# Layer 0 of a two-layer transformer in chunks of 2, 4, 4, 4 and 2 tiles, with held-back first loads and longer transfer latencies in the scheduler's model

## The chip, the cores and the metric

The kernel runs on one core of one Trainium2 chip. The metric is device time in microseconds (us) of one execution. A profile is one execution recorded by the hardware profiler. The engines carry these names in it: PE is TensorE doing matmuls, PEld is TensorE loading weights (the two overlap), DVE is VectorE, ACT is ScalarE, POOL is GpSimd, SP is SyncE. A name such as SPq means the instruction queue of that engine.

## The reference

Two layers, each with sliding-window attention and a feed-forward block, both behind a layer norm. There are 2048 tokens (16 tiles of 128), width 576, 32 heads of 18, a window of 256 keys and a feed-forward width of 4608. Both layers use the same weights, which are read in bfloat16.

```python
def _A_ref(x, wqkv, wo):                       # attention, H = 32, Dh = 18, W = 256
    q, k, v = split((x @ wqkv))
    scores = einsum("bhqd,bhkd->bhqk", q, k) * Dh ** -0.5
    mask = (i - j >= 0) & (i - j < W)
    p = softmax(where(mask, scores, -1e9))
    return (p @ v) @ wo
def _B_ref(x, w1, b1, w2, b2):                 # feed-forward
    return gelu(layernorm(x) @ w1 + b1) @ w2 + b2

x = x + _A_ref(_layernorm(x), wqkv, wo)        # layer 0
x = x + _B_ref(_layernorm(x), ...)
x = x + _A_ref(_layernorm(x), wqkv, wo)        # layer 1
x = x + _B_ref(_layernorm(x), ...)
```

## The kernel before

The kernel walks through chunks of four tiles, four chunks a layer, eight in all. In the step of chunk k, the attention of chunk k and the feed-forward of chunk k - 1 are written side by side, so that TensorE has feed-forward matmuls to do while ScalarE works on the exponentials of the attention.

```python
CH = [(l, t, 4) for l in range(NL) for t in range(0, NT, 4)]     # (layer, first tile, tiles)
...
for k in range(NK + 1):
    b = 4 * k                                      # a lower number is a higher priority
    if not last:
        if 0 < k < NK - 1: ln1(k + 1, b + 1)       # layer norm and transposes for the next qkv
        E(k, range(0, 4), b - 0.5)                 # attention, first half of the heads
    if k >= 2: mm2(k - 2, 1, b); w2_load(0, b + 1) # second-layer matmuls, two chunks back
    if k >= 1: G_part(k - 1, 0, b + 1)             # first-layer matmuls and gelu, first half
    if not last: E(k, range(4, 8), b + 1.5)
    if k >= 1: mm2(k - 1, 0, b + 2); w2_load(1, b + 3)
    if not last:
        ... qkv(k + 1, i, b + 2.2 + 0.2 * i) ...
        tail(k, b + 1.9)                           # transposes of the attention, output projection
    if k >= 1: G_part(k - 1, 1, b + 3)
```

This text does not fix the order in which an engine executes. Every `add(...)` makes a task with an engine, a `cost` (time on the engine), a `lat` (further time until its result may be read) and a priority. A list scheduler plays the program through on a model of the engines and writes one fixed order for each engine. On the chip an engine keeps this order and waits on semaphores where a result isn't there yet. So a wrong `lat` makes nothing incorrect; it makes the model believe that an instruction will not have to wait.

```python
# Plan.schedule, cut
for e in ENGS:
    for t in released[e]:
        st = max(free[e], t.ready)
        ...
        key = (round(st, 3), t.prio, t.idx)        # the earliest start wins, then the priority
...
t.end = st + t.cost + t.lat
s.ready = max(s.ready, st + t.cost + (t.lat if data and not same else 0.0))
```

Scores and first-layer matmuls keep the order of the text among themselves (`fifo="pa"`), and so do exp and gelu on ScalarE (`fifo="act"`). Second-layer matmuls, qkv and the output projection are free: they are the filler that the scheduler can put anywhere.

The parts that the change touches: the transposes, which are DMAs from on-chip memory to on-chip memory, issued by SyncE; the masks on GpSimd; and the loads at the start.

```python
# layer norm -> xnTa or xnTm; q and k -> qT and kT; attention -> attT
add("sp", lambda e: e.dma_start_transpose(dst[...], xn[:, sl, :]), ..., dma="t", cost=1.3, lat=1.4, prio=prio)
add("sp", lambda e, ...: e.dma_start_transpose(dst, qn[:, sl, :]), ..., dma="t", cost=1.3, lat=1.4, prio=prio)
add("sp", lambda e, i=i: e.dma_start_transpose(attT[...], attq[:, i, :]), ..., dma="t", cost=1.3, lat=1.4, prio=prio - 0.1)

# scores: one unit is four heads against up to 512 query columns; two exps, then the masks
add("act", lambda e, h2=h2: e.activation(pT[:, sl, 2*h2:2*h2+2, lo:hi], two(bs[h2])[:, :, lo:hi], ACT.Exp, scale=SCALE), ..., fifo="act")
ap = pT[:, sl, :, col:col + nb * 128]
add("pool", lambda e, ...: e.affine_select(ap, ap, pattern=pat, ...), ...)

# start: all weights and all of x at once; x as bfloat16, then 16 casts to the float32 residual
x_load(0, n0, [], 4.0, -10)
for n, w in enumerate("qkv"):
    dma("act", wqkv[...], A_wqkv[...], lat=7.0 + 3 * n, prio=-10, fifo="act")
for a in range(n0, NT, 4):
    x_load(a, min(4, NT - a), ["wkA"], ...)
dma("act", wo_sb[...], A_wo[...], lat=14.0, ...)
...
for t in range(NT):
    add("pool", lambda e, t=t: e.tensor_copy(x_res[:, t, :], x_in[:, t, :]), reads=[f"xin{t}"], writes=X(t), cost=0.7, ...)
for _ in range(NB1):
    w1_load(0, [f"q{n0 - 1}"])
w2_load(0, 0, [f"q{n0 - 1}"])
```

The softmax here doesn't subtract the row's maximum and nothing guards it: scores larger than these inputs give would overflow.

## Time and profile before

| | before |
|---|---|
| time, median of the first 3 runs | 1006.06 us (1005.98 to 1006.28) |
| span of the profiled run | 1007.7 us |
| TensorE busy | 927.4 us, 92% |
| first qkv matmul, first scores, first feed-forward matmul | 15.0, 34.0, 133.4 us |
| TensorE waits for the attention transposes | 16.8 us |
| moved by DMA | 126.60 MB |

From the page of the kernel before: busy time of each engine with its share of the span and its instruction count, then four rows in 40 slices of 25.2 us. A digit is the busy share in tenths; PEclk is the granted TensorE clock in tenths of full speed.

```profile
PE 927.4 (92%) x9312; PEld 584.9 (58%) x9312; DVE 311.9 (31%) x771; ACT 586.2 (58%) x705; POOL 378.4 (38%) x519
PE   3596799899999999899998999999999999999998
ACT  0356568577753777447761687627774377852531
PEclk9786799999999999999998999999999999999999
DMA  9925220974268251881628633484517725074540
```

TensorE bounds the kernel: from the sixth slice on its row is nearly all nines. The first five slices are different, with low digits and a low clock. That is the ramp. The windows view of the kernel before splits it. The columns are the stretch, its length, busy us (and instructions) of PE, PEld, DVE, ACT and POOL, the granted clock, the mean share of DMA engines in use, and GB/s.

```profile
0.00:34.00 34.00, 17.14 (x120) 12.47 (x121) 20.40 (x54) 1.28 (x1) 22.22 (x41) 1.00 1.24 231
34.00:80.00 46.00, 28.96 (x402) 18.70 (x402) 22.57 (x62) 27.26 (x37) 24.15 (x35) 0.78 0.53 142
80.00:92.00 12.00, 8.38 (x134) 4.97 (x134) 2.88 (x8) 8.56 (x12) 8.02 (x12) 0.53 0.62 88
92.00:120.00 28.00, 19.34 (x194) 11.68 (x195) 15.24 (x36) 13.36 (x14) 19.52 (x26) 0.65 0.43 85
120.00:160.00 40.00, 39.22 (x401) 23.18 (x400) 9.79 (x24) 28.57 (x35) 10.25 (x14) 1.00 0.23 65
```

Before 120 us TensorE is idle in part, and what it does runs at 0.53 to 0.78 of its clock for 86 us. A busy PE is therefore not enough as a measure. This document uses **lost time**: the length of a stretch minus the matmul work done in it, each matmul priced at its rate when TensorE runs without gaps. The prices come from the trace: 144 second-layer matmuls of 288 columns back to back took 17.64 us (0.1225 us each), 90 first-layer ones of 512 columns took 19.43 us (0.216 us), and other shapes are priced the same way by their columns (the 20-column value matmuls at 0.026 us, and the scores, four at a time on 32 rows each, at a quarter). Lost time adds up idle time and slow clock. It is an estimate, but with the same prices for every run. The kernel before loses 67.7 us by 130 us, a further 10.8 by 240 us, and 63.1 us in the 768 us after that.

The waits view of the kernel before, TensorE only. A line reads: what waited (written tile, source line), what ended the wait, us in all, times, longest. Line 519 is a qkv or output-projection matmul, 589 a score matmul, 598 an exp, 636 a value matmul, 619 a mask.

```profile
PE ps L519 <- DMA xnTa<-xn: 25.3, 4, 15.0
PE ps L519 <- DMA attT<-attq: 16.8, 9, 3.6
PE ps L589 <- ACT pT L598: 12.2, 22, 1.3
PE ps L636 <- POOL pT L619: 3.8, 5, 1.0
```

The second line is 16.8 us in nine waits, and it lies in the stage where TensorE is the bottleneck. One of the nine in the timeline of the kernel before (start, us, what, with the idle time before it in brackets):

```profile
298.38 0.29 PE L525 MATMUL ps<-wqkv,xnTa 128*128 128x288 bf16 x1
300.87 0.66 PE L519 MATMUL ps<-wo_sb,attT 128*128 128x288 bf16 x4 [2.19 <-DMA attT<-attq]
```

TensorE ends a qkv matmul and then sits for 2.19 us in front of the output projection, because the order says that the projection is next. The transpose needed 2.6, 3.2 and 5.9 us (least, median, most) from its issue to landing. The model has `cost` 1.3 and `lat` 1.4, together 2.7 us: nearly the least of the three.

### The profile page before, as it was taken

Reading aid. Unit: us, or ns where it says so; the run is one execution under the profiler, and the core shown is the slowest. Engines: PE = TensorE matmul, PEld = TensorE weight load, DVE = VectorE, ACT = ScalarE, POOL = GpSimd, SP = SyncE. Lnnn points to the kernel's source line nnn. Section 1 sums busy time; section 2 is a strip of 40 time slices with the busy share of each in tenths; the row PEclk is TensorE's granted clock in tenths of the full one; section 3 lists DMA queues with packets and bytes.
Section 4 is the critical chain, followed back from the end, with each engine's and each line's share of the span. In section 5 each row is a group of like instructions: output and inputs, shape, how many; then the busy total and the mean of one; then the engine's idle time right before and its main releaser. Section 6 shows DMA issues by size and latency. Waiting matters only on the chain.

```text
span 1007.7 us, 22352 instructions
## 1 busy us (share of the span) xinstructions
PE 927.4 (92%) x9312; PEld 584.9 (58%) x9312; DVE 311.9 (31%) x771; ACT 586.2 (58%) x705; POOL 378.4 (38%) x519
## 2 busy tenths in 40 slices
PE   3596799899999999899998999999999999999998
PEld 2363556556565656656575565755566565656556
DVE  4742611342136211534036130361114410132001
ACT  0356568577753777447761687627774377852531
POOL 8445724354333434425153161533333342541000
PEclk9786799999999999999998999999999999999999
DMA  9925220974268251881628633484517725074540
GB/s 252 273 45 89 54 72 25 199 187 131 72 150 164 75 163 39 180 184 41 183 70 170 148 108 94 120 177 103 166 48 170 143 66 183 25 194 122 184 129 25
DMA packets 226757, 126.60 MB, mean 126 GB/s; under 512 B 141792, under 2 KB 226528, under 8 KB 226656
## 3 DMA queue, kind: packets, MB, share of 16 engines
q1 hardware_dynamic: 219456, 122.20, 49.0%
q10 hardware_dynamic: 2432, 2.65, 0.9%
q0 software_dynamic: 4768, 0.31, 0.8%
q8 instruction: 74, 1.21, 0.5%
q14 instruction: 27, 0.22, 0.1%
HBM read 90.10 MB, written 2.36 MB: 92 GB/s over the span
## 4 chain that ended last, share of the span: by engine, by line
PE 68%; DMA 4%; DVE 3%; ACT 3%; issue 1%; POOL 1%; SPq 0%; DVEq 0%
PE ps L737 26%; PE ps L712 24%; PE ps L519 6%; PE ps L636 6%; PE ps L589 4%; DMA attT<-attq 3%; ACT pT L598 2%; PE ps L525 1%; DVE x_res L670 1%; DMA xnTm<-xn 1%; POOL rstd L460 1%; DVE xn L470 1%; ACT hT L716 1%; DVE st_all L447 0%; ACT L753 0%
## 5 line engine op out<-in xcount | busy, mean ns | idle before, releaser
L619 POOL TENSOR_SCALAR_AFFINE_SELECT pT<-pT 128x512 bf16<-128x512 bf16 (+1 forms) x368 | 278.1, 778 | 409.6 <-ACT pT L598 385.3
L598 ACT ACTIVATE pT<-ps 128x1024 bf16<-128x1024 f32 (+2 forms) x384 | 347.2, 971 | 133.6 <-PE ps L589 132.2
L716 ACT ACTIVATE hT<-ps,b1col 128x512 bf16<-128x512 f32 x288 | 196.6, 687 | 262.6 <-PE ps L712 262.4
L737 PE MATMUL ps<-w_sb,hT 128*128 128x288 bf16 x2304 | 314.2, 286 | 6.7 <-DVE x_res L670 5.6
L712 PE MATMUL ps<-xnTm,w_sb 128*128 128x512 bf16 x1440 | 320.1, 379 | 0.1
L737 PEld LDWEIGHTS ps<-w_sb,hT 128*128 128x128 bf16 x2304 | 210.3, 97 | 80.7 <-issue 20.5
L712 PEld LDWEIGHTS ps<-xnTm,w_sb 128*128 128x128 bf16 x1440 | 139.6, 98 | 158.6 <-issue 0.2
L670 DVE TENSOR_TENSOR x_res<-ps,x_res 128x288 f32<-128x288 f32 x160 | 71.0, 450 | 399.9 <-PE ps L737 362.4
L519 PE MATMUL ps<-wqkv,xnTa 128*128 128x288 bf16 x768 | 127.7, 297 | 29.7 <-DMA xnTa<-xn 25.3
L636 PEld LDWEIGHTS ps<-vA,pT 128*128 128x128 bf16 x2880 | 94.4, 96 | 29.1 <-issue 11.2
L519 PEld LDWEIGHTS ps<-wqkv,xnTa 128*128 128x128 bf16 x768 | 73.1, 101 | 58.5 <-issue 18.8
L636 PE MATMUL ps<-vA,pT 128*128 128x20 bf16 x2880 | 100.5, 172 | 5.3 <-POOL pT L619 3.8
L589 PE MATMUL ps<-qT,kT 32*128 32x384 bf16 (+2 forms) x1408 | 76.5, 285 | 18.7 <-ACT pT L598 12.2
L555 DVE CAST qn<-ps 128x288 bf16<-128x288 f32 x128 | 57.0, 452 | 55.2 <-PE ps L525 50.0
L519 PE MATMUL ps<-wo_sb,attT 128*128 128x288 bf16 x256 | 45.9, 313 | 16.8 <-DMA attT<-attq 16.8
L525 PE MATMUL ps<-wqkv,xnTa 128*128 128x288 bf16 x192 | 56.8, 296 | 0.0
L589 PEld LDWEIGHTS ps<-qT,kT 32*128 32x128 bf16 x1408 | 22.6, 93 | 53.9 <-issue 30.0
L694 POOL TENSOR_TENSOR x_res<-x_res,b2bc 128x576 f32<-128x576 f32 x32 | 45.0, 1409 | 15.1 <-DVE xn L470 13.9
L673 DVE TENSOR_TENSOR xn<-ps,x_res 128x288 bf16<-128x288 f32 x32 | 14.6, 457 | 114.7 <-PE ps L737 114.7
L470 DVE TENSOR_SCALAR xn<-x_res,mv_all,rstd 128x576 bf16<-128x576 f32 x60 | 43.1, 723 | 22.1 <-POOL rstd L460 10.4
L458 POOL TENSOR_SCALAR vtmp<-mv_all 128x1 f32<-128x1 f32 (+1 forms) x43 | 8.6, 200 | 103.6 <-DVE mv_all L449 101.2
L519 PEld LDWEIGHTS ps<-wo_sb,attT 128*128 128x128 bf16 x256 | 26.2, 106 | 30.7 <-DMA attT<-attq 20.6
(29 smaller groups left out, 281.5 us busy)
## 6 DMA issues: line engine op xcount, KB each, us to landing
w_sb<-in_B_w_dram SPq DMA_DIRECT2D x144, 288.0 KB, 5.2
w_sb<-in_B_w_dram SPq DMA_DIRECT2D x72, 512.0 KB, 4.2
w_sb<-in_B_w_dram SPq DMA_DIRECT2D x72, 64.0 KB, 3.9
hT<-in_A_x_dram SPq DMA_DIRECT2D x4, 576.0 KB, 6.3
out_dram<-xn SPq DMA_DIRECT2D x16, 144.0 KB, 1.8
wqkv<-in_A_wqkv_dram ACTq DMA_DIRECT2D x3, 576.0 KB, 7.4
wo_sb<-in_A_wo_dram ACTq DMA_DIRECT2D x1, 576.0 KB, 9.6
xnTa<-xn SPq DMA_TRANSPOSE x32, 3.9
```

Source lines behind the costliest of these rows:

```text
L470: add("dve", lambda e: e.tensor_scalar(xn[:, sl, 0:D], s[:, t, :], mv_all[:, t, 0:1], rstd[:, t:t + 1], op0=ALU.subtract, op1=ALU.mult), r ...
L519: ins = e.matmul(bank(bs[o])[:, 0:n], lhs(o, c, full), rhs(o, c, full), start=(c == 0), stop=False)
L525: ins = e.matmul(bank(bs[o])[:, 0:n], lhs(o, 4, full), rhs(o, 4, full), start=False, stop=True)
L555: add("dve", lambda e, o=o, b=bs[o], qv=qv: e.tensor_copy(qv[:, o * 16:(o + 1) * 16, 0:DH], bank(b)[:, 0:HB].rearrange("p (h d) -> p h d", ...
L589: ins = e.matmul(two(bs[j // 2])[:, j % 2, col:col + nq * 128], kT[32 * j:32 * j + 32, g, (T0 + so) % KS, :], qT[32 * j:32 * j + 32, g, qo ...
L598: add("act", lambda e, h2=h2: e.activation(pT[:, sl, 2 * h2:2 * h2 + 2, lo:hi], two(bs[h2])[:, :, lo:hi], ACT.Exp, scale=SCALE), reads=[bs ...
L619: add("pool", lambda e, ap=ap, pat=pat, sgn=sgn, kind=kind: e.affine_select(ap, ap, pattern=pat, compare_op=(ALU.is_ge if kind == "d" else ...
L636: ins = e.matmul(bank(B_O)[:, o:o + VW], pT[:, sl, j, col + qi * 128:col + (qi + 1) * 128], vA[:, (T0 + so) % VS, 4 * g + j, :], start=(fi ...
L670: add("dve", lambda e: e.tensor_tensor(x_res[:, t, sl], bank(b)[:, 0:HB], x_res[:, t, sl], ALU.add), reads=[b], writes=[f"x{t}h{hh}"], cos ...
L712: ins = e.matmul(bank(bk)[:, 0:n], w1_sb[:, sl, col:col + 128], xnTm[:, k % 2, c, 0:n], start=(c == 0), stop=(c == KD - 1))
L716: add("act", lambda e, f=f, fl=fl, bk=bk: e.activation(hT[:, fl, 0:n], bank(bk)[:, 0:n], ACT.Gelu_apprx_tanh, bias=b1col[:, f:f + 1]), rea ...
L737: ins = e.matmul(bank(b)[:, 0:HB], hT[:, fl, i * 128:(i + 1) * 128], w2_sb[:, fl, hh * HB:(hh + 1) * HB], start=(fl == 0), stop=(fl == NFH ...
```

## The change

The intent: start the first feed-forward earlier by making the first chunk smaller, give the first transposes a quieter DMA system, and let the scheduler see how slow transfers are. Four parts:

1. Layer 0 goes in chunks of 2, 4, 4, 4 and 2 tiles, nine chunks in all instead of eight.
2. The first loads are held back: Wv, Wo, W1, W2 and x beyond chunk 0 wait for steps of the ramp, and this x goes straight into the float32 residual by a converting DMA from GpSimd.
3. The model gives each DMA a share of the bandwidth (`dma_free`, `move`).
4. The model gives transposes a longer latency: 2.5 or 4.0 us instead of 1.4.

The diff also holds smaller edits (for example, a cheaper clearing of `qn` at the start and a later place for one bias addition on GpSimd). The diff, cut to its core:

```diff
-    CH = [(l, t, 4) for l in range(NL) for t in range(0, NT, 4)]
+    CH = [(0, t, n) for t, n in ((0, 2), (2, 4), (6, 4), (10, 4), (14, 2))] + [(1, t, 4) for t in range(0, NT, 4)]
...
             free[t.eng] = st + t.cost
+            if t.dma is not None:
+                dma_free = max(dma_free, st + t.cost) + t.move
+                t.lat = max(t.lat, dma_free + 1.3 - st - t.cost)
             t.end = st + t.cost + t.lat
...
-            reads=rd, writes=[f"{dname}{i}"], dma="t", ring=8, cost=1.3, lat=1.4, prio=prio)
+            reads=rd, writes=[f"{dname}{i}"], dma="t", ring=8, cost=1.3, lat=2.5, move=0.6, prio=prio)
...
-                    reads=[f"qn{sl}h0", f"qn{sl}h1"], writes=[dn], dma="t", ring=8, cost=1.3, lat=1.4, prio=prio)
+                    reads=[f"qn{sl}h0", f"qn{sl}h1"], writes=[dn], dma="t", ring=8, cost=1.3, lat=2.5, move=0.6, prio=prio)
...
-                reads=rd + ["aqd"], writes=[f"aT{i}"], dma="t", ring=8, cost=1.3, lat=1.4, prio=prio - 0.1)
+                reads=rd + ["aqd"], writes=[f"aT{i}"], dma="t", ring=8, cost=1.3, lat=4.0, move=0.6, prio=prio - 0.1)
...
-    for t in range(NT):
-        add("pool", lambda e, t=t: e.tensor_copy(x_res[:, t, :], x_in[:, t, :]), reads=[f"xin{t}"], writes=X(t), cost=0.7, ...)
+    x_load(CH[1][1], CH[1][2], [f"xa{n0 - 1}"], -6)      # chunk 1, after the last transpose of chunk 0
+    w_load(2, ["xa0"])                                   # Wv, after the first transpose
     for i in range(n0):
         qkv(0, i, -5)
-    for _ in range(NB1):
-        w1_load(0, [f"q{n0 - 1}"])
-    w2_load(0, 0, [f"q{n0 - 1}"])
+    x_load(0, n0, [f"k{n0 - 1}"], -4)
...                                                       # Wo, W1, W2 and later x after steps of attention 0
```

## The prediction

> **What bounds it now.** TensorE: 927 of 1007.7 us busy (busy table). From 126 us on, windows of about 119 us per four-tile chunk hold 110 to 117 us of matmul work at granted clock 0.97 to 1.00. The exception is the ramp. Before 126 us no feed-forward matmul runs: TensorE shows 79.8 us busy, but much of it at half clock (windows: 0.78 at 34-80 us, 0.53 at 80-92, 0.65 at 92-120). Priced at full-clock rates (144 second-layer matmuls take 17.64 us, so 0.1225 us each; 90 first-layer ones take 19.43; a chunk's attention about 20.7 us by subtraction in the 245-365 us window), the work done by 126 us (303 qkv and 40 output-projection matmuls, a little over one chunk's scores and values) is worth about 64 us. So the ramp loses about 60 us: 15 us until the first transpose lands, 7.8 us more at 44-52 us waiting for a transpose stuck behind 13 weight issues, then attention alone, bound by exp and mask and slowed clock. Low clock fits the Trainium skill, "TensorE: Matmul & The Clock Gate", Part 1: an idling array falls to half clock; the trace's 0.53 agrees.
>
> **What the change does.**
> 1. Chunk 0 has two tiles: 8 score units of 384 columns (1.51 us exp each) instead of 24 units (about 36 us of exp); two tiles of transposes instead of four at each step.
> 2. Holding back Wv, x, Wo, W1, W2 frees the DMA engines, saturated for the first 40 us (252, 273 GB/s in the slices), so first transposes land in about 3.5 us instead of 5.4.
> 3. x goes straight into the float32 residual by converting GpSimd DMA, removing 16 casts (9.8 us GpSimd). That only GpSimd DMA converts is from the skill, "DMA: Bandwidth & Descriptors", SWDGE vs HWDGE vs iDMA; no run here shows it yet.
> 4. Cost: a ninth pass over W1 and W2, 10.6 MB (126.6 to about 136 MB), 36 more gelus (estimate 0.47 us each, from 0.687 at 512 columns and exp's column rate; about +8 us ScalarE), and 360 matmuls of 256 columns in place of 180 of 512: about even, 0.11 us each by estimate, perhaps +1 to 3 us. Stages pairing four-tile attention with a two-tile feed-forward carry about 68 us ScalarE beside 77 us TensorE: estimate 4 us loss in each of two.
> 5. The longer transpose latency in the model should move filler work before the output projection, which waits 16.8 us in all for its transposes (waits): estimate 5 us gained.
>
> **On the critical path.** Estimate: first qkv at 11-12 us (was 15.0), first scores at 22-25 (34.0), attention 0 ends near 39, feed-forward starts at 55-62 us (was after 126), with about 39 us of full-clock work done by then. Ramp loss falls from 60 to about 20 us: 40 gained, 8 given back in two-tile stages, 2 in narrow matmuls, 3 in DMA contention there, plus 5 to 10 from the schedule. The final 96 us, pure feed-forward, stay.
>
> Predicted: 968 us, 80% between 948 and 984. Faster by over 2%: 0.88; within 2%: 0.10; slower: 0.02.
>
> **Right if** the first first-layer matmul starts at 55-65 us; TensorE idle before 130 us falls from 46 to about 20 us; granted clock is near 1.00 from 65 us; 245-1008 us pace is unchanged; waits for the attention transposes fall. **Wrong if** converting x loads land late, so qkv of chunk 1 can't fill attention 0 (feed-forward still starts, but attention 1 trails: 10-15 us lost); if weights can't keep up with two-tile feed-forwards (waits on W1 or W2 DMAs near 60-120 and 540 us); if the new order leaves larger waits in steady stages; if ScalarE binds those stages.

## The result and the profile after

| | before | after |
|---|---|---|
| median of 4 runs | 1006.02 us (1003.86 to 1006.28) | 995.85 us (991.85 to 997.73) |
| span of the profiled run | 1007.7 us | 995.1 us |
| first qkv, scores, feed-forward matmul | 15.0, 34.0, 133.4 us | 12.6, 26.1, 84.7 us |
| lost by 130 us | 67.7 us | 63.3 us |
| lost by 240 us | 78.5 us | 71.6 us |
| lost after 240 us | 63.1 us | 57.7 us |
| moved by DMA | 126.60 MB | 139.91 MB |

The ratio is 0.9898, with a 95% interval of 0.9864 to 0.9933: about 1% faster, which counts as within 2%. A ratio here is the mean time of one kernel's fast runs over that of the other's fast runs of the same rounds, so it is not quite the ratio of the medians that are quoted. The predicted 968 us and even the upper end of its range, 984, are missed.

The same rows of the page after:

```profile
PE 923.4 (93%) x9513; PEld 602.7 (61%) x9556; DVE 320.4 (32%) x787; ACT 601.1 (60%) x745; POOL 370.5 (37%) x506
PE   4757799999899999999999999998999999999998
ACT  0458638777477837552677577856775387852531
PEclk9777799999999999999999999999999999999999
DMA  9966599226924293619366953196526716074540
```

The ramp is still five slices long, and the clock in it is no better. (TensorE's count of matmul records is lower than that of weight loads, because some matmul records are missing from this trace; lost time uses the weight loads for the first layer.) The windows of the kernel after:

```profile
34.00:60.00 26.00, 22.93 (x264) 16.79 (x261) 17.98 (x53) 6.17 (x9) 6.67 (x11) 0.91 1.33 231
60.00:80.00 20.00, 9.61 (x198) 5.17 (x199) 7.79 (x17) 18.23 (x20) 18.64 (x25) 0.56 0.24 56
80.00:92.00 12.00, 10.94 (x146) 8.14 (x143) 3.75 (x8) 9.04 (x14) 6.15 (x9) 0.73 0.60 117
92.00:126.00 34.00, 27.32 (x338) 18.24 (x336) 8.86 (x28) 24.58 (x31) 17.18 (x24) 0.80 0.70 201
126.00:160.00 34.00, 32.36 (x336) 25.85 (x335) 21.88 (x52) 16.73 (x27) 13.62 (x18) 1.00 1.05 217
```

The stretch from 60 to 80 us is the centre of the miss. It is attention of chunk 1, four tiles, and TensorE is busy for 9.61 of 20 us at 0.56 of its clock, while GpSimd has 18.64 us of work (13.8 of it masks, the rest bias additions and layer norm) and ScalarE (the exps) 18.23. TensorE has nothing but scores and values in its order there. Three rows of the timeline after show the marks that the prediction named:

```profile
59.42 0.40 PE L593 MATMUL ps<-qT,kT 32*128 32x384 bf16 x8
84.73 2.60 PE L716 MATMUL ps<-xnTm,w_sb 128*128 128x256 bf16 x15
89.13 7.80 PE L716 MATMUL ps<-xnTm,w_sb 128*128 128x256 bf16 x70
```

The first scores of chunk 1 come at 59.4 us, and the first feed-forward matmul at 84.7, behind the first half of that attention. Then 70 narrow matmuls run in 7.80 us, 0.111 us each, so narrow matmuls as such cost nothing extra.

The waits of TensorE after (line 523 is the old 519, 593 the old 589, 640 a value matmul, 623 a mask):

```profile
PE ps L523 <- DMA xnTa<-xn: 13.2, 2, 12.6
PE ps L593 <- ACT pT L602: 12.6, 22, 1.7
PE ps L640 <- POOL pT L623: 11.9, 12, 2.3
PE ps L523 <- DMA attT<-attq: 8.4, 8, 2.9
```

The wait for the layer-norm transposes fell by 12.1 us and that for the attention transposes by 8.4; waits for the masks rose from 3.8 to 11.9 us. Two rivals for the 1% were on the table now. Theory A: the chunks gave most of the gain in the ramp and later stages gave part of it back. Theory B: the chunks gave nothing, and the gain is the scheduler's latency. A third question was what kept the ramp loss at 63 us.

### The profile page after: what moved, and what is told of

Read it like the earlier page. It is cut to its first block, busy times and chain, and to the rows that moved or that the text cites. A ratio compares the mean times of both kernels' runs of the same rounds, so it can differ in the third digit from the quotient of the medians.

```text
span 995.1 us, 22912 instructions
## 1 busy us (share of the span) xinstructions
PE 923.4 (93%) x9513; PEld 602.7 (61%) x9556; DVE 320.4 (32%) x787; ACT 601.1 (60%) x745; POOL 370.5 (37%) x506
## 2 busy tenths in 40 slices
DMA packets 237415, 139.91 MB, mean 141 GB/s; under 512 B 142400, under 2 KB 235136, under 8 KB 237312
## 3 DMA queue, kind: packets, MB, share of 16 engines
q0 software_dynamic: 6896, 5.03, 2.8%
## 4 chain that ended last, share of the span: by engine, by line
PE 80%; DMA 7%; POOL 3%; DVE 3%; issue 2%; ACT 2%; SPq 2%; POOLq 0%; DVEq 0%
PE ps L741 27%; PE ps L716 27%; PE ps L523 11%; PE ps L640 7%; PE ps L593 5%; DMA attT<-attq 3%; PE ps L529 3%; POOL pT L623 2%; DMA xnTm<-xn 2%; ACT pT L602 2%; DVE x_res L674 1%; SPq L406 1%; SPq L566 1%; DMA xnTa<-xn 1%; POOL rstd L464 1%
## 5 line engine op out<-in xcount | busy, mean ns | idle before, releaser
L720 ACT ACTIVATE hT<-ps,b1col 128x512 bf16<-128x512 f32 (+1 forms) x324 | 205.9, 639 | 228.8 <-PE ps L716 224.3
L741 PE MATMUL ps<-w_sb,hT 128*128 128x288 bf16 x2304 | 320.0, 290 | 11.6 <-DVE x_res L674 7.1
L716 PE MATMUL ps<-xnTm,w_sb 128*128 128x512 bf16 (+1 forms) x1577 | 315.4, 355 | 2.9 <-ACT pT L602 0.6
L741 PEld LDWEIGHTS ps<-w_sb,hT 128*128 128x128 bf16 x2304 | 213.1, 99 | 87.6 <-issue 19.5
L716 PEld LDWEIGHTS ps<-xnTm,w_sb 128*128 128x128 bf16 x1620 | 157.3, 98 | 145.0 <-issue 0.4
L523 PE MATMUL ps<-wqkv,xnTa 128*128 128x288 bf16 x768 | 124.8, 292 | 14.6 <-DMA xnTa<-xn 13.2
L640 PE MATMUL ps<-vA,pT 128*128 128x20 bf16 x2880 | 101.4, 172 | 12.0 <-POOL pT L623 11.9
L523 PEld LDWEIGHTS ps<-wqkv,xnTa 128*128 128x128 bf16 x768 | 71.4, 99 | 40.2 <-issue 14.1
L593 PE MATMUL ps<-qT,kT 32*128 32x256 bf16 (+2 forms) x1472 | 78.2, 286 | 18.7 <-ACT pT L602 12.6
L451 DVE BATCH_NORM_STATS2 st_all<-x_res 128x6 f32<-128x288 f32 x124 | 52.4, 445 | 13.9 <-DMA x_res<-in_A_x_dram 12.6
L529 PE MATMUL ps<-wqkv,xnTa 128*128 128x288 bf16 x192 | 56.0, 292 | 0.0
L462 POOL TENSOR_SCALAR vtmp<-mv_all 128x1 f32<-128x1 f32 (+2 forms) x42 | 8.3, 198 | 119.7 <-DVE mv_all L453 117.6
L523 PE MATMUL ps<-wo_sb,attT 128*128 128x288 bf16 x256 | 40.1, 286 | 8.5 <-DMA attT<-attq 8.4
L677 DVE TENSOR_TENSOR xn<-ps,x_res 128x288 bf16<-128x288 f32 x32 | 14.6, 458 | 97.8 <-PE ps L741 97.8
```

Of the source, the lines that this page charges most:

```text
L451: add("dve", lambda e, i=i, s=s: e.bn_stats(st_all[:, t, i, :], s[:, t, i * HB:(i + 1) * HB]), reads=res, writes=[f"st{t}_{i}"], cost=0.43 ...
L523: ins = e.matmul(bank(bs[o])[:, 0:n], lhs(o, c, full), rhs(o, c, full), start=(c == 0), stop=False)
L529: ins = e.matmul(bank(bs[o])[:, 0:n], lhs(o, 4, full), rhs(o, 4, full), start=False, stop=True)
L593: ins = e.matmul(two(bs[j // 2])[:, j % 2, col:col + nq * 128], kT[32 * j:32 * j + 32, g, (T0 + so) % KS, :], qT[32 * j:32 * j + 32, g, qo ...
L640: ins = e.matmul(bank(B_O)[:, o:o + VW], pT[:, sl, j, col + qi * 128:col + (qi + 1) * 128], vA[:, (T0 + so) % VS, 4 * g + j, :], start=(fi ...
L716: ins = e.matmul(bank(bk)[:, 0:n], w1_sb[:, sl, col:col + 128], xnTm[:, k % 2, c, 0:n], start=(c == 0), stop=(c == KD - 1))
```

## The experiments

Seventeen kernels ran, in five jobs after the first. Each job had its own runs of the kernel before, whose median lay between 1004.3 and 1008.8 us, so ratios are the safer comparison across jobs. The kernel after was not run again in them. The table of lost time at the end of this section puts all of the runs side by side.

### Which part of the change gives the time

**Chunks alone, and the rest alone.** The first is the kernel before with only the line `CH` of the change. The second is the kernel after with the old line.

```diff
 # chunks only: before
-    CH = [(l, t, 4) for l in range(NL) for t in range(0, NT, 4)]
+    CH = [(0, t, n) for t, n in ((0, 2), (2, 4), (6, 4), (10, 4), (14, 2))] + [(1, t, 4) for t in range(0, NT, 4)]
 # rest only: after, with that line put back
```

> The kernel before with one line changed: layer 0 in chunks of 2, 4, 4, 4, 2; loads, gates and scheduler model as before. Theory T1 (what the ramp loses is the attention of the first four-tile chunk that no feed-forward work can fill; shrinking chunk 0 shortens attention 0 by some 24 us of exp but the next attention is then unfilled in its place): a small gain, 1000 to 1006 us. Rival T2 (the small chunks alone gain the 40 us of the prediction and something else in the change gives them back): 965 to 980 us. Rival T3 (two-tile chunks cost by themselves through the ninth weight pass): over 1008 us.

> The changed kernel with layer 0 back in four chunks of four tiles; held-back loads, converting loads and the new scheduler model stay. T1: the holding back and the model are worth 5 us or less together: 1000 to 1008 us. T2 (the rest of the change loses what the chunks gain): 1020 us or more. T3 (the rest gains, the chunks lose): under 995 us.

Measured: chunks alone 1012.47 us (1012.0 to 1015.17), ratio 1.0041 [1.0019, 1.0063]: no gain, but a small loss. The rest alone 990.74 us (989.05 to 991.37), ratio 0.9817 [0.9797, 0.9837]: more than the gain of the whole change (0.9898 [0.9864, 0.9933], from the first job). So the headline of the change, the chunk sizes, is not where the time came from. Chunks alone started the feed-forward at 99.8 us and lost 58.7 us by 130 us against 67.7 in the kernel before, but by 240 us they had lost 77.4 against 78.5. What the ramp gained was lost again at once. So both totals lie in the range of T3, but within the ramp the chunks behave as T1 has it.

**The rest, with the old latency of transposes.** This is the previous kernel with the three transposes back at 1.4 us and without their share of bandwidth.

```diff
-  ... dma="t", ring=8, cost=1.3, lat=2.5, move=0.6 ...    (twice; and lat=4.0 once)
+  ... dma="t", ring=8, cost=1.3, lat=1.4 ...
-            if t.dma is not None:
+            if t.dma is not None and t.dma != "t":
```

> The four-tile kernel with the rest of the change (990.7 us), with the scheduler model's transposes put back to the old 1.4 us and no bandwidth share; loads keep the new model. If the longer transpose latency in the model is what gains 16 us after 130 us: time lost by TensorE after 130 us rises from 57 to about 70 us, its waits for the attention transposes from 2.3 to about 15 us, total 1000 to 1006 us. Rival (the held-back loads and the bandwidth share of loads gain it): 988 to 994 us.

Measured: 1008.33 us (1005.63 to 1011.21), ratio 1.0003 [0.9977, 1.0029]. The whole gain is gone, somewhat more than expected. The waits view has the reason. Rest only, then rest only with the old latency:

```profile
PE ps L523 <- DMA attT<-attq: 2.3, 3, 1.5
```

```profile
PE ps L523 <- DMA attT<-attq: 15.6, 9, 3.7
```

The nine waits are back. This run also says that held-back loads and the bandwidth in the model gain nothing without the latency.

**The latency alone, on the kernel before.** The first kernel has three changed numbers, the second one.

```diff
 # three numbers
-  xnT: lat=1.4      qT, kT: lat=1.4      attT: lat=1.4
+  xnT: lat=2.5      qT, kT: lat=2.5      attT: lat=4.0
 # one number
-  attT: lat=1.4
+  attT: lat=4.0
```

> The kernel before with three numbers of its scheduler model changed and nothing else: the latency that it reckons for transposes, 1.4 us, becomes 2.5 us (activations, q, k) and 4.0 us (attention). If these numbers are the whole gain of the rest of the change (17 us): 988 to 994 us, waits for the attention transposes 16.8 to under 4 us. If the bandwidth share or the held-back loads are needed beside them: 996 to 1004 us.

> The kernel before with one number changed: the model's latency of the attention transposes, 1.4 to 4.0 us. If the gain is the output projection's wait alone: 989 to 996 us, like the run with all three. If the longer latency of the q, k and activation transposes matters as much: 997 to 1004 us.

Measured: three numbers 992.92 us (990.87 to 993.12), ratio 0.9879 [0.9861, 0.9897]; one number 995.69 us (994.66 to 996.27), ratio 0.9911 [0.9891, 0.9931]. A single number in the scheduler's model gives as much as the whole change. The waits for the attention transposes fell to 1.8 us in both. The groups view in the stretch from 480 to 602 us shows what such a wait costs beside itself; after the name, the columns are busy us, mean ns of one matmul, and idle us before the group. First the kernel before, then the one with one number changed:

```profile
L519 PE MATMUL ps<-wo_sb,attT 128*128 128x288 bf16 x32 | 7.2, 366 | 3.6 <-DMA attT<-attq 3.6
```

```profile
L519 PE MATMUL ps<-wo_sb,attT 128*128 128x288 bf16 x32 | 5.0, 286 | 0.7 <-DMA attT<-attq 0.7
```

The matmuls after a wait of 3.6 us took 366 ns instead of 286: the granted clock was halved for 6.8 us, from 534.6 us on. Other waits of the kernel before show that the length of the wait alone does not decide this. Stretches from 245 to 365 us and from 720 to 880 us:

```profile
L519 PE MATMUL ps<-wo_sb,attT 128*128 128x288 bf16 x32 | 5.0, 286 | 2.2 <-DMA attT<-attq 2.2
```

```profile
L519 PE MATMUL ps<-wo_sb,attT 128*128 128x288 bf16 x32 | 6.6, 343 | 2.0 <-DMA attT<-attq 2.0
```

After 2.2 us the clock stayed whole, as it did after 3.2 us near 195 us; after 2.0 us it was halved for 3.4 us, from 776.9 us on. By the Trainium skill, "TensorE: Matmul & The Clock Gate", Part 1 (The HAM clock gate), the array falls to half its clock after an idle window of about 3.4 us. The 3.6 us wait agrees with that, the 2.0 us wait does not. A wait can be paid twice, then, but these traces give no length from which it is.

The transposes themselves became no faster (issue to landing 2.6, 3.0 and 5.7 us with three numbers changed). The scheduler now puts filler work, above all qkv of the next chunk, ahead of the output projection.

### Why the smaller first chunk did not shorten the ramp

**x of chunk 1 not held back.** The kernel after loads x of chunk 1 only when the last transpose of chunk 0 has landed. GpSimd issues the load, and its queue waits twice in front of x loads; then VectorE waits for the data. Timeline of GpSimd and one line of VectorE's waits, kernel after:

```profile
16.23 0.75 POOL L406 DMA_DIRECT2D x_res<-in_A_x_dram  x1 [5.63 <-DMA xnTa<-xn]
26.25 0.70 POOL L406 DMA_DIRECT2D x_res<-in_A_x_dram  x1 [9.27 <-DMA kT<-qn]
DVE st_all L451 <- DMA x_res<-in_A_x_dram: 12.6, 1, 12.6
```

So qkv of chunk 1 started at 34.7 us and could not fill attention 0. The experiment issues both loads at the start.

```diff
-    x_load(CH[1][1], CH[1][2], [f"xa{n0 - 1}"], -6)
-    x_load(0, n0, [f"k{n0 - 1}"], -4)
     w_load(0)
     w_load(1)
+    x_load(CH[1][1], CH[1][2], [], -10)
+    x_load(0, n0, [], -9)
```

It was run on the kernel after and on the four-tile version.

> The changed kernel with the converting loads of x for chunks 0 and 1 issued at the start, not after the first transposes and keys. If holding back chunk 1's x is itself a cost (it landed at 23 us, its transposes at 34.5, and its first scores could only start at 59.4): qkv of chunk 1 starts by 23 to 26 us instead of 34.7, first scores of chunk 1 by 48 to 52, total 984 to 990 us. If the bandwidth that it frees for Wq and Wk matters more: first matmul later than 12.6 us by 2 us or more and total 995 us or more.

> The four-tile kernel with the rest of the change (990.7 us), with x of chunks 0 and 1 loaded at once. If holding x back costs here as it did with two-tile chunks (4 to 5 us): 984 to 988 us. If attention 0 of four tiles is so long that chunk 1's x is never awaited: 989 to 993 us.

Measured: on the kernel after 991.0 us (989.39 to 992.37), ratio 0.9822 [0.98, 0.9843]; on four tiles 989.31 us (988.24 to 991.95), ratio 0.9818 [0.9797, 0.9839]. With the early load the new chunks are 4.9 us faster in the medians of two jobs (995.85 to 991.0, just above the expected range), and the old chunks are no faster. The windows of the kernel after with the early load:

```profile
60.00:80.00 20.00, 19.46 (x267) 13.39 (x265) 14.12 (x34) 13.57 (x14) 14.08 (x19) 0.99 0.36 61
```

TensorE is busy for 19.46 us of the same 20, at full clock, because qkv of chunk 2 now falls into attention 1. Yet the sum of the time is only level with the four-tile version: the lost time by 130 us falls from 63.3 to 56.3 and the lost time from 130 to 240 us rises from 8.3 to 14.1. So only 1.2 us of the gain lie before 240 us. The other 5.0 us of the two profiles lie after it, and the half exps below show that such a difference can come without any edit. Even mended, the new chunks gain nothing over the old.

**What bound attention 1: masks, exps, or both.** Three kernels that give wrong results. One masks only a quarter of the elements in chunk 1, one takes the exp of only half the columns in chunk 1, one does both. Apart from one clearing of a buffer the instructions stay the same, and TensorE's order does.

```diff
 # quarter masks in chunk 1
             ap = pT[:, sl, :, col:col + nb * 128]
+            if k == 1:
+                pat = [[0, 1]] + pat[1:]
+                ap = pT[:, sl, 0:1, col:col + nb * 128]
 # half exps in chunk 1 (pT is cleared once at the start)
-  e.activation(pT[:, sl, 2*h2:2*h2+2, lo:hi], two(bs[h2])[:, :, lo:hi], ...)
+  he = hi if k != 1 else lo + (hi - lo) // 2
+  e.activation(pT[:, sl, 2*h2:2*h2+2, lo:he], two(bs[h2])[:, :, lo:he], ...)
```

> Wrong result on purpose: the changed kernel, same instruction order on every engine, with the GpSimd masks of chunk 1 run on a quarter of their elements. If the masks bound attention 1 (GpSimd was busy 18.6 of 20 us at 60-80 us): the stretch from 59 to 85 us shrinks by 5 us or more and the total to 983 to 988 us. If exp on ScalarE bounds it: under 3 us, 992 to 996 us.

> Wrong result on purpose: the changed kernel, same instruction order, exp of chunk 1 on half of its columns (a clearing of the probabilities' buffer at the start is added). If exp bounds attention 1: TensorE's loss between 60 and 130 us falls from 32 to under 20 us and the total to 980 to 985 us. If the masks alone bound it (a quarter of the masks had taken 7 us off that loss): under 3 us gained, 993 to 997 us. If both work in turn on one chain of three buffers: about 5 to 8 us each, 987 to 991 us.

> Wrong result on purpose: the changed kernel, same order, chunk 1 with masks on a quarter of the elements and exp on half of the columns. TensorE's loss by 240 us was 71.6 with neither, 64.2 with short masks, 71.4 with short exp. If masks bind first and exp directly behind them: 50 to 58 us, total 975 to 983 us. If short masks had already left the fixed order and the transposes as the limit: 61 to 65 us, 985 to 989 us.

Measured: quarter masks 987.86 us (983.85 to 996.4, a wide range), ratio 0.9806 [0.9746, 0.9867]; half exps 991.57 us (990.52 to 995.27), ratio 0.9843 [0.9818, 0.9868]; both 987.21 us (987.13 to 987.57), ratio 0.9799 [0.9773, 0.9825]. The same stretch of the windows view in four kernels: the kernel after, then quarter masks, then half exps, then both.

```profile
72.00:84.00 12.00, 7.83 (x148) 4.21 (x144) 5.34 (x9) 9.93 (x11) 11.74 (x15) 0.50 0.31 42
```

```profile
72.00:84.00 12.00, 9.94 (x152) 6.48 (x149) 4.02 (x9) 11.71 (x15) 5.26 (x13) 0.60 0.45 57
```

```profile
72.00:84.00 12.00, 8.26 (x153) 4.53 (x154) 5.65 (x9) 5.44 (x11) 11.85 (x16) 0.50 0.27 42
```

```profile
72.00:84.00 12.00, 10.93 (x165) 6.45 (x165) 4.01 (x9) 9.05 (x16) 5.94 (x16) 0.51 0.42 66
```

With full masks GpSimd (fifth figure) is full, 11.74 of 12 us, whether the exps are whole or halved. With quarter masks GpSimd has room and ScalarE (fourth) becomes full at 11.71. So the masks on GpSimd bind here first, and once they are short ScalarE is full. In lost time by 130 us, quarter masks are worth 6.9 us (63.3 to 56.4) of the 32.0 that this stage loses from 60 to 130 us, half exps nothing (63.6), and both together no more than the masks alone (56.5; 63.8 by 240 us, as its second case expected). So there is a further limit: with both relieved, TensorE shows as busy for 10.93 of 12 us, but at 0.51 of its clock. From 60 to 130 us TensorE's idle time falls from 18.1 us in the kernel after to 9.3 with both, but some 14 us are lost to slow matmuls in either. Why the clock stays low there is not shown by a run. The loss by 130 us stays at 56 us, so even an attention 1 with far less work on GpSimd and ScalarE leaves most of the predicted gain missing.

The half exps also show how far a total can be trusted. By 240 us that kernel loses as much as the kernel after (71.7 and 71.6), and its TensorE order is the same throughout, yet its median is 4.3 us lower and falls in none of the expected ranges. The difference lies after 240 us (55.2 against 57.7 in the profiles), where the edit does not reach. So a difference of 4 to 5 us between the total of the kernel after and one from a later job is no evidence by itself; the lost time of the ramp is.

**Quarter masks on four tiles** (chunks 0 and 1, wrong), to see whether the masks are a matter of the new chunks.

```diff
 # rest only
+            if k < 2:
+                pat = [[0, 1]] + pat[1:]
+                ap = pT[:, sl, 0:1, col:col + nb * 128]
```

> Wrong result on purpose: the four-tile kernel with the rest of the change, same order, masks of chunks 0 and 1 on a quarter of the elements. Its loss by 240 us was 72.5. If the masks on GpSimd hold the ramp at four tiles as at two: 60 to 66 us, total 978 to 985 us. If they hold only the chunked kernel: 70 to 73 us, 988 to 992 us.

Measured: 987.55 us (984.52 to 988.76), ratio 0.9796 [0.9768, 0.9824]; rest only had 0.9817. So 5 us less are lost by 130 us (63.4 to 58.2) and 2 to 4 in the whole; 68.8 us by 240 us lies between the two expected ranges. The masks cost something in the ramp of the four-tile version too, not only with the new chunks.

**A real cure for the masks: every second one on VectorE,** as a multiply with a tile of zeros and ones. The result is right. Both kernels have the early x load.

```diff
+            if k < 2 and mi % 2 == 1:
+                add("dve", lambda e, a4=a4, mb=mb: e.tensor_tensor(a4, a4, mb, ALU.mult), ...)
+                continue
             add("pool", lambda e, ...: e.affine_select(...))
```

> The four-tile kernel with the rest of the change and early x (989.3 us), with every second mask of chunks 0 and 1 done on VectorE by a multiplication with a 0/1 tile; the result stays right. If GpSimd's masks bound the attention of the ramp: TensorE's loss before 130 us falls from 63.5 to 52 to 58 us and the total to 979 to 985 us. If exp is next at once, or VectorE's own queue stalls: 986 to 992 us.

> The same masks on the kernel with chunks of 2, 4, 4, 4, 2 and early x (991.0 us). A quarter of the masks in chunk 1 had gained 8 us: so 983 to 987 us here, and still not below the four-tile kernel with the same masks, as the two-tile chunk at the layer boundary costs 7 us. If small chunks pay once the masks no longer bind: under 980 us.

Measured: four tiles 994.66 us (993.64 to 995.76), ratio 0.9901 [0.9883, 0.9919]; new chunks 993.36 us (992.21 to 996.12), ratio 0.9892 [0.987, 0.9914]. Without the moved masks the ratios were 0.9818 and 0.9822, so by the ratios of two jobs this is a loss of 0.7 to 0.8%, a miss; of lost time the profiles differ by 1.7 and 1.2 us only. By 130 us nothing was gained on the new chunks (55.9 against 56.3 us lost) nor on four tiles (63.6 both); some 3 us more were lost later on four tiles. In the median a mask took 0.43 us on VectorE against 0.64 on GpSimd, but the medians hide what happens when both engines work at masks. GpSimd's masks in the first 130 us, new chunks with early x, then the same with every second mask on VectorE (busy us, mean ns, idle before):

```profile
L625 POOL TENSOR_SCALAR_AFFINE_SELECT pT<-pT 128x512 bf16<-128x512 bf16 x45 | 28.3, 644 | 38.6 <-ACT pT L604 34.1 <-PE ps L642 4.2
```

```profile
L636 POOL TENSOR_SCALAR_AFFINE_SELECT pT<-pT 128x512 bf16<-128x512 bf16 x23 | 19.5, 846 | 46.4 <-ACT pT L609 43.8 <-PE ps L653 2.6
```

A mask on GpSimd now took 846 ns in the mean instead of 644 (866 for the 21 that ran beside a mask of VectorE, 637 for the other two), and one on VectorE 570. GpSimd's busy time still fell, from 65.1 to 50.7 us, while VectorE's rose from 61.0 to 78.8. So 14 us less on GpSimd with 18 us more on VectorE gained nothing. VectorE also does the copies out of TensorE's accumulators; whether these came late is not shown by a run.

**The feed-forward ahead of attention 1.** Perhaps only the order was at fault: the first half of feed-forward 0 stands behind the first half of attention 1. This moves it ahead, on the kernel after, on the kernel after with early x, and on four tiles.

```diff
+            if k == 1:
+                G_part(0, 0, b - 1)
             E(k, range(0, 4), b - 0.5)
...
-        if k >= 1:
+        if k >= 2:
             G_part(k - 1, 0, b + 1)
```

> The changed kernel with one block moved: the first half of chunk 0's first feed-forward layer stands ahead of the first half of attention 1 in the order that both share, not behind it. If that order is what held the feed-forward back from the predicted 55-62 us to 84.7: it starts at 66 to 72 us, TensorE's loss before 130 us falls from 63 to 50 to 56 us, total 984 to 990 us. If the order only decides which of two idle stretches comes first, as the attention's exp and masks have to be waited for anyway: it starts as early, but the loss by 240 us stays at 69 to 74 us and the total at 993 to 998 us.

> The same move with x of chunks 0 and 1 loaded at once (991.0 us without the move). If order and late x cost separately: 978 to 984 us. If early x had already filled attention 1 with chunk 2's qkv, so that both gains are the same idle time: 988 to 993 us.

> The same move on the four-tile kernel with the rest of the change (990.7 us). If the order costs there too: loss before 130 us from 63 to 52 to 58 us, total 980 to 987 us. If attention 0's 24 units and not the order set that ramp: 988 to 993 us.

Measured: 997.26 us (996.67 to 998.36), ratio 0.9888 [0.986, 0.9916]; with early x 998.23 us (997.43 to 1002.09), ratio 0.9901 [0.9871, 0.9932]; on four tiles 1000.73 us (1000.47 to 1002.04), ratio 0.9921 [0.9897, 0.9945]. The first is as its second case expected; the two others are slower than their ranges. In the first, the feed-forward started at 65.0 us, near the 55 to 62 that was predicted, and the lost time by 130 us fell to 58.5. But the total is unchanged: by 240 us it had lost 73.9 against 71.6. Its waits view has a new line for the first-layer matmuls:

```profile
PE ps L716 <- DMA xnTm<-xn: 7.9, 1, 7.9
```

TensorE now stands still for 7.9 us for the last transposes before the feed-forward, and it still waits 9.6 us in all for masks (11.9 in the kernel after). An early feed-forward is a mark, not a gain: the filler is spent earlier and missing later. On the versions that were already good this order lost about 1%.

### What the two-tile chunks cost later

**Chunks of 2, 2, 4, 4, 4,** with early x. Here no two-tile chunk stands at the layer boundary.

```diff
-    ((0, 2), (2, 4), (6, 4), (10, 4), (14, 2))
+    ((0, 2), (2, 2), (4, 4), (8, 4), (12, 4))
```

> The kernel a3 (changed kernel, x of chunks 0 and 1 loaded at once; 991.0 us) with layer 0 in chunks of 2, 2, 4, 4, 4. Theory: the ramp loses in attention 1 because a four-tile attention (47 us of exp) stands against two tiles of feed-forward; with two tiles it is 24 us of exp, and no two-tile chunk is left at the layer boundary, where 560-720 us lost 6 us more than the four-tile kernel: 978 to 985 us. Rival (two feed-forward passes of two tiles in a row starve on weight loads, 21 MB in some 100 us, or the attention of chunk 2 is then as unfilled): 990 us or more.

Measured: 994.22 us (992.42 to 996.8), ratio 0.987 [0.9842, 0.9898], against 0.9822 for 2, 4, 4, 4, 2 with early x. Its loss by 130 us, 53.1, is the lowest of all runs. But from 130 to 240 us it loses 21.8 us instead of 14.1. On the other hand the stretch from 560 to 720 us, the layer boundary, loses 10.8 us, as four tiles do (10.3 with the rest only), where every kernel with a two-tile chunk at the end of layer 0 loses 15.0 to 19.6. In the kernel after, TensorE's longest wait in that stretch is for a residual addition on VectorE:

```profile
PE ps L741 <- DVE xn L677: 3.8, 1, 3.8
PE ps L523 <- DMA attT<-attq: 3.0, 3, 1.3
```

The rest only has 0.6 and 1.5 us there. So a two-tile feed-forward beside a four-tile attention costs 5 to 8 us at the layer boundary (16.1 against 10.9 with early x, 17.9 against 10.3 without), and some 8 from 130 to 240 us when it is moved into the ramp, less the 3 that this kernel gains before 130 us. That the pairing is the reason there is argued; no run isolates it. Placing the chunk elsewhere did not remove the cost.

### Lost time of all runs

Us, by the definition above, from the profiled run of each kernel. The part at 560 to 720 us is contained in the column before it.

| kernel | ratio to before | lost by 130 us | by 240 us | after 240 us | 560 to 720 us |
|---|---|---|---|---|---|
| before | 1 | 67.7 | 78.5 | 63.1 | 12.5 |
| after | 0.9898 | 63.3 | 71.6 | 57.7 | 17.9 |
| chunks only | 1.0041 | 58.7 | 77.4 | 69.3 | 19.6 |
| rest only | 0.9817 | 63.4 | 72.7 | 48.5 | 10.3 |
| rest, old latency | 1.0003 | 64.6 | 77.4 | 65.8 | 13.3 |
| before, three latencies | 0.9879 | 67.6 | 75.1 | 48.0 | 10.7 |
| before, one latency | 0.9911 | 71.5 | 78.5 | 48.8 | 11.4 |
| after, early x | 0.9822 | 56.3 | 70.4 | 52.7 | 16.1 |
| rest, early x | 0.9818 | 63.6 | 75.3 | 49.0 | 10.9 |
| 2, 2, 4, 4, 4, early x | 0.9870 | 53.1 | 74.9 | 49.4 | 10.8 |
| after, quarter masks (wrong result) | 0.9806 | 56.4 | 64.2 | 55.0 | 16.0 |
| after, half exps (wrong result) | 0.9843 | 63.6 | 71.7 | 55.2 | 17.3 |
| after, both (wrong result) | 0.9799 | 56.5 | 63.8 | 54.9 | 15.0 |
| rest, quarter masks (wrong result) | 0.9796 | 58.2 | 68.8 | 47.9 | 10.2 |
| rest, early x, VectorE masks | 0.9901 | 63.6 | 73.8 | 52.2 | not read |
| after, early x, VectorE masks | 0.9892 | 55.9 | 70.2 | 54.1 | 16.9 |
| feed-forward first | 0.9888 | 58.5 | 73.9 | 54.2 | 17.3 |
| feed-forward first, early x | 0.9901 | 58.4 | 74.6 | 54.5 | 16.6 |
| rest, feed-forward first | 0.9921 | 65.1 | 83.5 | 49.3 | 11.4 |

Read the column after 240 us: with the new latency and no two-tile chunk at the boundary it is 48 to 52, with the old latency 63 to 69, with the new latency and a two-tile chunk at the boundary 53 to 58. That last difference is for the most part the price of this chunk, as the column at 560 to 720 us shows. The column by 240 us falls no lower than 70 in any kernel with a right result, however early the feed-forward begins.

## Why the prediction was wrong

**The step that failed** is the sum for the ramp, "Ramp loss falls from 60 to about 20 us: 40 gained". The loss by 130 us went from 67.7 to 63.3 us, and chunks alone, carried to 240 us, gained 1.1 us of 78.5. The step under it is the overlap, in the pairing of a four-tile attention with a two-tile feed-forward: "estimate 4 us loss in each of two". Counting ScalarE's 68 us beside TensorE's 77 us assumed that the two can run side by side. In the stage of attention 1 of the kernel after (60 to 130 us) the loss is 32.0 us, about what attention 0 with its 30.2 us cost in the same stretch of the kernel before, and eight times the estimate. Before 60 us the loss fell only from 37.5 to 31.3 us. Shown by runs: three quarters of GpSimd's masks cost 7 us of that stage, and with them short neither the exps nor the masks set its length (quarter masks, half exps, both); putting the feed-forward ahead doesn't pay (feed-forward first); the held-back x costs 7 us by 130 us, but only 1.2 by 240 (early x). These overlap, and the larger part of the 32.0 us stays unexplained. Argued from the code, and consistent with all of this: a two-tile chunk 0 also leaves only half the feed-forward work to fill the four-tile attention 1, and first-layer matmuls and gelus keep a fixed order with scores and exps, so they can't be filler inside a half of an attention. That the prediction counted only ScalarE in this stage and left out GpSimd was part of the error: the windows before had both nearly equal in attention 0 (27.26 and 24.15 us of 46, then 8.56 and 8.02 of 12).

**The term that was mis-sized low** is the schedule, "estimate 5 us gained", from the waits of 16.8 us. The direction and the mechanism were right (the sum on the critical path has "plus 5 to 10" for it). Measured alone on the kernel before, the three latencies gave 1.2%, about 12 us; taken out of the four-tile version, they cost 17.6 us (990.74 to 1008.33, in two jobs whose kernels before had medians of 1008.61 and 1008.81). Two parts were missing from the estimate: nearly all of the 16.8 us went, and slow clock behind some of the waits went with it (10.2 us at half clock after 240 us in the kernel before, none with the rest only until its last matmul). After 240 us, TensorE was idle for 25.5 us in the kernel before and 15.3 with the rest only, while lost time fell by 14.6; so 10 us are idle time and some 4 us slower work.

**The price of two-tile stages**, "8 given back", was too small at the boundary: 5 to 8 us at 560 to 720 us for one such stage, against the predicted 4. With the chunks alone it cost 7.1 us (19.6 against 12.5), more than the 1.1 us that they had gained by 240 us.

**What was right, or nearly.** The first qkv matmul was predicted at 11 to 12 us and came at 12.6; the first scores at 22 to 25, came at 26.1; the exps of attention 0 ended at 42.9, predicted near 39. The first layer-norm transpose was predicted to land in 3.5 instead of 5.4 us and took 5.0, so most of the earlier start came from elsewhere: the norm of the first tile was ready 2.2 us earlier. A gelu of 256 columns took 473 ns, predicted 0.47 us. Narrow matmuls came out even. The feared waits for weights didn't come: no line of TensorE's waits in the kernel after names a weight load, although 13.3 MB more were moved (predicted about 10). That x loads land late, the first item under "wrong if", did happen; its cost, 7 us by 130 us and 1.2 by 240, is below the predicted 10 to 15. That x is converted on the way is in the profile after: the software queue of GpSimd moved 5.03 MB instead of 0.31. It agrees with the Trainium skill, "DMA: Bandwidth & Descriptors", SWDGE vs HWDGE vs iDMA, by which a cast during a DMA is only possible from GpSimd. The waits for the attention transposes fell, as predicted, though only by half in the kernel after. Two marks of the prediction showed it wrong from the profile alone: TensorE's idle time before 130 us went from 46.4 to 42.4 us, not to 20, and the granted clock was predicted near 1.00 from 65 us and got there at about 120.

**What stays open.** On top of the latency, the held-back loads, the saved casts and the bandwidth in the model seem to give a little (0.9817 for the rest against 0.9879 for the latency alone, in different jobs; 990.74 against 992.92 us in the medians). By themselves they give nothing (1.0003). Which of them works with the latency was not separated. At least 53 us of loss by 130 us remain in every kernel; some 30 of them fall before 60 us, in the chain of load, norm, transpose, qkv, transpose and scores.

The best right versions are the four-tile chunks with the rest of the change, with or without early x, at 989 to 991 us, and the new chunks with early x, at 991.0. All three have lower ratios than the kernel after (0.9817 to 0.9822 against 0.9898).

## What to carry to other kernels

Where a list scheduler writes a fixed order, compare its latencies with the landing times in a trace first: one number, 1.4 to 4.0 us, was worth as much here (0.9911) as the whole change with its new ramp (0.9898), because TensorE waited in front of work that other work could have preceded. A smaller first chunk makes the next stage start earlier, but, as argued above, it also halves the filler that this stage has to offer, so price the stage after it by its own bottleneck engine (here GpSimd and ScalarE, not TensorE) and don't take an earlier start for a gain. The Trainium skill says in "Perfetto Trace Analysis", Optimization Strategy, that kernels whose most contended engine changes over time may gain from interleaving these regimes; early x agrees within its stretch (TensorE 19.46 instead of 9.61 of 20 us beside the masks), but by 240 us it gained only 1.2 us: work that is moved forward is missing later.

## What the Trainium skill lacked or had wrong

- "DMA: Bandwidth & Descriptors" has a rate for DMA transposes, but no time from issue to landing for a small one from on-chip memory to on-chip memory. "VectorE: DVE Perf Modes", The three transpose paths, has 1309 ns for 128 by 128 by DMA, without saying from where to where it counts. In the kernel before an attention transpose of 128 by 640 bfloat16 took 2.6 us at least, 3.2 in the median and 5.9 at most, and held SyncE's queue for 1.27 us (median).
- "GPSIMD Engine Reference" has no time for an affine select as a mask. On 128 by 512 bfloat16 it took 0.64 us in the median, and a VectorE multiply of that shape 0.43; with both engines at masks they were slower, 0.85 and 0.57 in the mean.
- "TensorE: Matmul & The Clock Gate", Part 1, names an idle window of about 3.4 us for the fall to half clock. In the kernel before the clock fell after a wait of 2.0 us and not after one of 3.2 us, so the length of one wait did not predict it.
- "DMA: Bandwidth & Descriptors" says which engine can convert during a DMA, but has no landing time for such a load beside other traffic: in the kernel after, the three larger ones (1152 KB as the profile counts them) took 8.3 us in the median.
